# A second seven-product set in the first layer of a retention and feed-forward kernel on one Trainium2 core

## Chip, cores and metric

The kernel runs on one core of one Trainium2 chip. The metric is the device time of one execution in microseconds (us). Of the kernel before, ten executions are known.

## What is computed

A retention (linear attention with decay) over 8 batches, 8 heads, 576 positions and 64 dimensions gives a matrix of 4608 tokens by 512; a two-layer feed-forward net with a leaky ReLU of slope 0.01 follows.

```
scores = scale * q @ k.T            # per batch and head
ret    = (scores * Dmat) @ v        # Dmat = gamma_h ** (row - col), 0 above the diagonal
x      = ret, heads side by side    # (4608, 512)
h      = x @ w_in                   # (512, 2048)
g      = maximum(0.01 * h, h)
out    = g @ w_out                  # (2048, 512), float32
```

## The kernel before

**Tiling.** The 4608 tokens are 36 units of 128 tokens, or nine groups `g` of 512 tokens, four units each. The retention is done per unit `u` in two chunks of 64 positions: scores inside a chunk (masked), and a state matrix that is carried from chunk to chunk. There are nine chunks in a batch; chunk number 2u or 2u+1 modulo 9 says what `state` has to do: 0 is a copy, 8 is nothing, 3 and 7 take an addition and a scaling, the others one addition. In f16, TensorE does all the products.

**The order of the work is written by hand.** Every engine carries out its instructions in the order of the program's text; the code issues pieces of retention between pieces of the feed-forward net. `burst(u)` issues the scores of unit u and the outputs of unit u-1 on TensorE, then the evacuations: `masks` (VectorE, scores from PSUM times the mask, to f16), `state` (VectorE), `state_cast` (GpSimd), `own` (ScalarE) and `add` (VectorE), which give the columns `xT` of the net's input. `step(u)` is a burst, the loads of unit u+4 on SP's DMA queue, and `ahead(u+2)`: casts of k on ScalarE, of q and v on GpSimd, and the transposing DMA on SP. Once in a group `step` also has `sum_x`, four differences of `xT` on GpSimd.

**First layer.** A block `f` is 128 of the 2048 hidden columns for the group's 512 tokens: `h_block`, four matmuls of 512 columns into one PSUM buffer, then `leaky` on ScalarE. For the set of blocks 0, 1, 8 and 9 of groups 2 to 8, `h_seven` (from line 447) uses a Strassen-like scheme: a 2x2 split of the weights, of the contraction and of the tokens, with seven products of four 256-column matmuls in place of four blocks of four 512-column matmuls. It needs the sums of weights `w_sum` (made once by `sum_w_in` on VectorE), the sums of inputs from `sum_x`, and additions on VectorE (`plus`, line 468: `u2`, `v`, `h4`, `h5` and a second `h4`). Its first product `p1` is copied by ScalarE to `k1` (line 475), and then `p1` goes on accumulating in the same PSUM buffer. Four plain blocks, given in `fill`, lie between the products. I write p1b, p5b and p7b for the second product that goes into the buffer p1, p5 or p7.

**Second layer.** `seven` has the same scheme, each product 16 matmuls of 256 columns. Its sums of activations are made by `mix` on VectorE in 16 bits (line 554): four kinds, each for two halves `x` of the hidden columns; kinds 2 and 3 are written in place. Its p1 is copied to `k1` by ScalarE in `keep` (line 586), and `give` (line 600) adds and stores. The results of a product are written to SBUF tiles and go out by SP.

**Order in a group before the change:** `h_seven` with four plain blocks, a step, six plain blocks (with three mixes of half 0 after the third), a step, two plain blocks, three mixes of half 1, and then `seven`: p1, two mixes, a step, p1b, p6, p5, p7, a step, p5b, p7b. All products of both layers use one pool `acc` of four PSUM buffers, which are taken in turn; scores (`sc`) and outputs (`ot`) have a buffer each of their own. `m_pool` holds the copies and sums with one buffer for each name.

**Ahead of the groups**, units 0 to 7 are brought in with finer pieces: transposes of q and k on TensorE, which `turn` copies from PSUM by VectorE and `turn_act` by ScalarE (line 208). Group 0 is done without the scheme (`wide`), group 1 with the second layer's alone (`seven(1, ...)`).

Of the kernel before, what the change touches and what calls it, by code (L numbers as in the profile page):

```python
# [18 lines left out]
def kernel(  # L19
# [9 lines left out]
    nc = tc.nc  # L29
# [74 lines left out]
    w_in16 = const_pool.tile([P, NP, DFF], F16, name="w_in16")  # L104
    w_out16 = const_pool.tile([P, NF, DM], F16, name="w_out16")
    w_mix = const_pool.tile([P, 4, HF, HN], F16, name="w_mix")
    w_sum = const_pool.tile([P, 4, NP // 2, 2 * P], F16, name="w_sum")
    zst = const_pool.tile([P, NP, CH], F16, name="zst")
    idle = const_pool.tile([P, TOK], F16, name="idle")

    t32, qk16, v16, qkT, s16s, st16, sc_tiles, ot_tiles, xT = ({} for _ in range(9))
    last_load = {}
# [119 lines left out]
                        start=True, stop=True, skip_group_check=True,  # L232
                    )

    def masks(u):
        s16s[u] = b_pool.tile([P, 2, NP, CH], F16, name="s16")
        nc.vector.tensor_tensor(  # L237
            out=s16s[u],
            in0=sc_tiles[u][:, :, 0],
            in1=mask_sb.unsqueeze(1).unsqueeze(1).to_broadcast([P, 2, NP, CH]),  # L240
            op=MUL,
        )
# [145 lines left out]
    def g_tile(g):  # L388
        if g not in g_t:
            g_t[g] = g_pool.tile([P, NF, TOK], F16, name="gt")  # L390
        return g_t[g]

    def leaky(out, in_):
        nc.scalar.activation(out=out, in_=in_, func=mybir.ActivationFunctionType.Lrelu)  # L394

    def h_block(g, f):
        hps = acc_pool.tile([P, 1, TOK], FP, name="acc")
        h_mm(hps, 0, g, f, slice(0, TOK))
        leaky(g_tile(g)[:, f : f + 1, :], hps)
# [15 lines left out]

    def w_sub(i, j):
        return w_in16[:, 2 * j : 2 * j + 2, i * HF * P : i * HF * P + 2 * P]

    def x_sub(g, j, k):
        return xT[g][:, 2 * j : 2 * j + 2, k * HT : (k + 1) * HT]

    def sum_w_in(n):
        a, b, op = (
            (w_sub(1, 0), w_sub(1, 1), ADD),
            (w_sum[:, 0], w_sub(0, 0), SUB),
            (w_sub(0, 0), w_sub(1, 0), SUB),
            (w_sub(0, 1), w_sum[:, 1], SUB),
        )[n]  # L430
        nc.vector.tensor_tensor(out=w_sum[:, n], in0=a, in1=b, op=op)

    x_sums = {}

# [9 lines left out]
        ):  # L444
            nc.gpsimd.tensor_tensor(out=t[:, n], in0=a, in1=b, op=SUB)  # L445

    def h_seven(g, fill):

        r = {}
        t = x_sums[g]  # L450

        def product(name, lhs, rhs, fresh):
            if fresh:
                r[name] = acc_pool.tile([P, 2, HT], FP, name="acc")
            for n in range(2):
                for c in range(NP // 2):
                    nc.tensor.matmul(  # L457
                        out=r[name][:, n, :],
                        lhsT=lhs[:, c, n * P : (n + 1) * P],
                        rhs=rhs[:, c, :],  # L460
                        start=fresh and n == 0 and c == 0,
                        stop=c == NP // 2 - 1,
                        skip_group_check=True,
                    )

        def plus(name, a, b):
            r[name] = m_pool.tile([P, 2, HT], FP, name=name)
            nc.vector.tensor_tensor(out=r[name], in0=r[a], in1=r[b], op=ADD)  # L468

        def give(i, k, name):  # L470
            leaky(g_tile(g)[:, i * HF : i * HF + 2, k * HT : (k + 1) * HT], r[name])

        product("p1", w_sub(0, 0), x_sub(g, 0, 0), True)
        r["k1"] = m_pool.tile([P, 2, HT], FP, name="k1")
        nc.scalar.copy(out=r["k1"], in_=r["p1"])
        h_block(g, fill[0])
        product("p1", w_sub(0, 1), x_sub(g, 1, 0), False)
        give(0, 0, "p1")
        h_block(g, fill[1])
        product("p6", w_sum[:, 1], t[:, 1], True)  # L480
        plus("u2", "p6", "k1")
        product("p5", w_sum[:, 0], t[:, 0], True)
        plus("v", "p5", "u2")
        h_block(g, fill[2])
        product("p7", w_sum[:, 2], t[:, 2], True)
        plus("h4", "p7", "v")
        product("p5", w_sum[:, 3], x_sub(g, 1, 1), False)
        plus("h5", "p5", "u2")
        give(1, 1, "h4")
        h_block(g, fill[3])  # L490
        give(0, 1, "h5")
        product("p7", w_sub(1, 1), t[:, 3], False)
        plus("h4", "p7", "u2")
        give(1, 0, "h4")

# [28 lines left out]
    def w_part(a, b):  # L524
        return w_out16[:, a * HF : (a + 1) * HF, b * HN : (b + 1) * HN]
# [13 lines left out]
    def g_part(g, a, b):  # L539
        return g_t[g][:, b * HF : (b + 1) * HF, a * HT : (a + 1) * HT]  # L540
# [12 lines left out]
        )[n]  # L553
        nc.vector.tensor_tensor(out=z[:, fs], in0=a[:, fs], in1=b[:, fs], op=op)  # L554

    def seven(g, hooks, last=False):

        r = {}
        s = sums[g]

        def product(name, lhs, rhs, fresh):
            apart = last and name == "p7"
            if fresh:
                r[name] = [
                    acc_pool.tile([P, 1 if apart else 2, HN], FP, name="acc")
                    for _ in range(2 if apart else 1)
                ]
            order = (
                [(f, tb) for tb in range(2) for f in range(HF)]
                if last  # L570
                else [(f, tb) for f in range(HF) for tb in range(2)]
            )
            for n, (f, tb) in enumerate(order):
                nc.tensor.matmul(  # L574
                    out=r[name][tb][:, 0, :] if apart else r[name][0][:, tb, :],
                    lhsT=lhs[:, f, tb * P : (tb + 1) * P],
                    rhs=rhs[:, f, :],
                    start=fresh and (f == 0 if apart else n == 0),
                    stop=f == HF - 1,
                    skip_group_check=True,  # L580
                )

        def keep(name, of, plus=None):
            r[name] = m_pool.tile([P, 2, HN], FP, name=name)
            if plus is None:
                nc.scalar.copy(out=r[name], in_=r[of][0])  # L586
            else:
                nc.vector.tensor_tensor(out=r[name], in0=r[of][0], in1=r[plus], op=ADD)

        def give(a, b, of, plus=None):  # L590
# [21 lines left out]
            if r["n", a] == 2 and not (last and a == 1):  # L612
                store(g, a, r["o", a])

        plan = (
            ("p1", g_part(g, 0, 0), w_part(0, 0), True, lambda: keep("k1", "p1")),
            ("p1", g_part(g, 0, 1), w_part(1, 0), False, lambda: give(0, 0, "p1")),
            ("p6", s[:, 1], w_mix[:, 1], True, lambda: keep("u2", "p6", "k1")),
            ("p5", s[:, 0], w_mix[:, 0], True, lambda: keep("v", "p5", "u2")),
            ("p7", g_part(g, 1, 0), w_mix[:, 2], True, lambda: give(1, 1, "p7", "v")),  # L620
            ("p5", g_part(g, 0, 0), w_part(1, 1), False, lambda: give(0, 1, "p5", "u2")),
            ("p7", g_part(g, 1, 1), w_mix[:, 3], False, lambda: give(1, 0, "p7", "u2")),
        )
        if last:
            plan = (plan[0], plan[2], plan[1]) + plan[3:]
        for n, (name, lhs, rhs, fresh, then) in enumerate(plan):
            product(name, lhs, rhs, fresh)
            then()
            if n == 0:
                mix(g, 3, 0)  # L630
                mix(g, 3, 1)
            for f in hooks.get(n, ()):
                f()

# [126 lines left out]
    def burst(u, out=True):  # L763

        if u < NU:
            scores(u)
        if out:
            outputs(u - 1)
        if u < NU:
            masks(u)  # L770
            state(u, 0)
            state(u, 1)
            state_cast(u, pool_copy)
        if out:
            own(u - 1)
            add(u - 1)
# [62 lines left out]
    masks(6)  # L839
    cast_q(7, nc.vector)  # L840
    state(6, 1)
    cast_v(7, nc.vector)
    h_unit(5, 1)
    turn(7, 1)
    halves(1, (0, 4))
    outputs(6)
    own(6)
    turn(7, 0)
    add(6)
    state_cast(6, act_copy, (1,))  # L850
    halves(1, (0, 5))
# [27 lines left out]
    def early(u, n):  # L879
# [7 lines left out]
        3: lambda: mixes(1, 1),  # L887
        4: lambda: (burst(8, False), ahead(11), load(13)),
        7: lambda: mixes(1, 2),
        12: lambda: [sum_w_in(n) for n in range(4)],  # L890
        9: lambda: early(9, 12),
    }
    for n in range(16):
# [1 line left out]
        if n in at:  # L895
            at[n]()
    burst(10)
    seven(1, {0: [lambda: early(11, 13)], 4: [lambda: early(12, 14)]})

    rest = [f for i in range(2, HF) for f in (i, i + HF)]  # L900
    for g in range(2, NG):
        more = g < NG - 1
        h_seven(g, rest[:4])
        if more:
            step(4 * g + 5)
        for n, f in enumerate(rest[4:]):
            h_block(g, f)
            if n == 2:
                for m in range(3):
                    mix(g, m, 0)  # L910
            if more and n == 5:
                step(4 * g + 6)
        for m in range(3):
            mix(g, m, 1)
        seven(
            g,
            {0: [lambda: step(4 * g + 7)], 4: [lambda: step(4 * g + 8)]} if more else {},
            g == NG - 1,
        )


# [28 lines left out]
```

## Time and profile before

| what | value |
|---|---|
| median of 10 executions | 287.45 us |
| lowest, highest | 287.18, 290.26 us |
| profiled execution, its own time | 288.79 us |
| its span in the profile | 287.0 us |
| TensorE clock granted, mean | 0.994 of full speed |
| groups 2 to 7 in the profile | five of 28.80 to 28.86 us, the first (84.32 to 113.20) 28.88 |
| group 8 (from 257.34 us) | to the end, 29.7 us |

The profile is of one execution, the median of ten others. The rows in order of time give start, length, engine, line, operation, the tile written and the tiles read, shapes and how many instructions were merged into the row; in brackets stands the idle time of the engine ahead of it and what ended that. A matmul's length in the rows is longer than its spacing from the next, since matmuls are pipelined; spacing is taken from starts. PE is TensorE, DVE VectorE, ACT ScalarE, POOL GpSimd.

### The profile page before, as it was taken

To read this page: it belongs to the slowest core of one execution; us is meant where nothing else is said; L and a number is where in the kernel's file an instruction comes from. 1 tells how busy PE (TensorE), PEld (TensorE's weight loads), DVE (VectorE), ACT (ScalarE), POOL (GpSimd) and SP (SyncE) were. 2 spreads that over 40 slices of the span, in tenths; PEclk is the share of its full clock that TensorE was granted. 3 is DMA by queue.
4 is the path that set the end of the run, shared out by engine and by line. 5 is a ranking of instruction groups with operands and counts; after the bars stand their busy time and mean duration, and the time that the engine had idled before them with its cause. 6 is when DMAs were issued, how large, how long until landed. Compare 5 with 4: busy or idle time off the path is not lost.

```text
span 287.0 us, 9702 instructions
## 1 busy us (share of the span) xinstructions
PE 277.6 (97%) x4195; PEld 198.6 (69%) x4195; DVE 204.8 (71%) x336; ACT 145.0 (51%) x261; POOL 141.1 (49%) x152
## 2 busy tenths in 40 slices
PE   5989999999999999999999999999999999999994
PEld 1558888745886588658865886588648864886584
DVE  1785577958766896699668975997599659845352
ACT  3567776623327832783278326832683167316610
POOL 8979402483446536553656446545655564132000
PEclk9799999999999999999999999999999999999999
DMA  8999999699999997948894969478959351012004
GB/s 217 299 234 229 287 207 234 154 190 234 243 222 282 214 204 165 276 106 173 184 274 97 206 148 276 110 168 185 255 127 174 76 185 39 3 49 100 0 0 148
DMA packets 131739, 50.03 MB, mean 174 GB/s; under 512 B 121264, under 2 KB 126000, under 8 KB 131696
## 3 DMA queue, kind: packets, MB, share of 16 engines
q1 hardware_dynamic: 125392, 39.59, 60.5%
q0 software_dynamic: 6016, 9.70, 15.0%
q8 instruction: 33, 0.54, 0.8%
q10 hardware_dynamic: 288, 0.11, 0.1%
q14 instruction: 10, 0.08, 0.1%
HBM read 36.81 MB, written 9.44 MB: 161 GB/s over the span
## 4 chain that ended last, share of the span: by engine, by line
PE 91%; DVE 3%; ACT 2%; DMA 2%; issue 1%; SPq 0%; ACTq 0%; DVEq 0%
PE acc L380 35%; PE acc L574 34%; PE acc L457 8%; PE acc L510 5%; PE sc L219 2%; DMA t<-in_q_dram 2%; PE ot L295 1%; PE ot L306 1%; PE sc L228 1%; PE acc L640 1%; PE acc L201 1%; ACT k L586 1%; ACT qkT L208 1%; PE acc L328 1%; DVE qk L176 0%
## 5 line engine op out<-in xcount | busy, mean ns | idle before, releaser
L380 PE MATMUL acc<-xT,w_in 128*128 128x512 f16 (+2 forms) x656 | 110.5, 317 | 0.4 <-ACT xT L348 0.3
L394 ACT ACTIVATE gt<-acc 128x512 f16<-128x512 f32 x123 | 71.4, 597 | 28.3 <-PE acc L380 27.8
L380 PEld LDWEIGHTS <-w_in 128*128 128x128 f16 x656 | 57.2, 98 | 34.0 <-issue 0.4
L574 PEld LDWEIGHTS <-gt 128*128 128x128 f16 x640 | 61.7, 98 | 9.5
L277 POOL CAST st<-s 128x512 f16<-128x512 f32 x21 | 12.8, 610 | 68.7 <-DVE s L261 40.5
L574 PE MATMUL acc<-w_out,gt 128*128 128x256 f16 x384 | 45.9, 273 | 0.4
L176 POOL TENSOR_TENSOR qk<-t,cs 128x512 f16<-128x512 f32 x28 | 32.5, 1162 | 20.2 <-DMA t<-in_q_dram 19.5
L362 ACT COPY own<-ot 128x512 f32<-128x512 f32 x33 | 19.2, 581 | 42.6 <-PE ot L306 36.5
L180 POOL TENSOR_TENSOR v<-t,cs 128x512 f16<-128x512 f32 x28 | 34.8, 1242 | 0.0
L574 PE MATMUL acc<-w_mix,gt 128*128 128x256 f16 x256 | 30.6, 273 | 0.0
L574 PE MATMUL acc<-w_mix,mix 128*128 128x256 f16 x256 | 29.6, 273 | 0.0
L574 PEld LDWEIGHTS <-mix 128*128 128x128 f16 x256 | 24.9, 98 | 3.2 <-DVE mix L554 0.2
L237 DVE TENSOR_TENSOR s<-sc,cs 128x512 f16<-128x512 f32 x34 | 23.2, 682 | 5.0 <-PE sc L228 5.0
L367 DVE TENSOR_TENSOR xT<-ot,own 128x512 f16<-128x512 f32 x33 | 22.6, 683 | 5.1 <-ACT own L362 5.1
L173 ACT CAST qk<-t 128x512 f16<-128x512 f32 x36 | 22.3, 620 | 4.6 <-DMA t<-in_k_dram 4.6
L554 DVE TENSOR_TENSOR mix<-gt 128x1024 f16<-128x1024 f16 x16 | 14.4, 904 | 7.8 <-ACT gt L394 7.8
L554 DVE TENSOR_TENSOR mix<-mix,gt 128x1024 f16<-128x1024 f16 x16 | 18.9, 1188 | 0.5
L445 POOL TENSOR_TENSOR x_sum<-xT 128x512 f16<-128x512 f16 x14 | 16.1, 1153 | 5.6 <-DVE xT L367 5.6
L261 DVE TENSOR_TENSOR s<-sc,s 128x256 f32<-128x256 f32 x37 | 15.5, 419 | 2.8 <-PE sc L228 2.2
L468 DVE TENSOR_TENSOR u<-acc,k 128x512 f32<-128x512 f32 x7 | 4.8, 691 | 17.1 <-PE acc L457 17.1
L600 DVE TENSOR_TENSOR osb<-acc,u 128x512 f32<-128x512 f32 (+1 forms) x17 | 11.2, 656 | 7.9 <-PE acc L574 7.9
L445 POOL TENSOR_TENSOR x_sum<-xT,x_sum 128x512 f16<-128x512 f16 x14 | 16.2, 1154 | 0.5
(74 smaller groups left out, 351.8 us busy)
## 6 DMA issues: line engine op xcount, KB each, us to landing
out_dram<-osb SPq DMA_DIRECT2D x17, 512.0 KB, 3.7
t<-in_k_dram SPq DMA_DIRECT2D x27, 256.0 KB, 4.0
t<-in_q_dram SPq DMA_DIRECT2D x26, 256.0 KB, 4.2
t<-in_v_dram SPq DMA_DIRECT2D x25, 256.0 KB, 4.5
w_in<-in_moe_w_in_dram POOLq DMA_DIRECT2D x8, 256.0 KB, 6.0
w_out<-in_moe_w_out_dram POOLq DMA_DIRECT2D x4, 512.0 KB, 10.1
t<-in_v_dram POOLq DMA_DIRECT2D x7, 256.0 KB, 5.7
t<-in_q_dram POOLq DMA_DIRECT2D x6, 256.0 KB, 5.6
```

Source lines behind the costliest of these rows:

```text
L173: nc.scalar.copy(out=qk16[u][:, 1], in_=t32[u, 1])
L176: eng.tensor_tensor(out=qk16[u][:, 0], in0=t32[u, 0], in1=decay(u, 0), op=MUL)
L180: eng.tensor_tensor(out=v16[u], in0=t32[u, 2], in1=decay(u, 1), op=MUL)
L237: nc.vector.tensor_tensor(out=s16s[u], in0=sc_tiles[u][:, :, 0], in1=mask_sb.unsqueeze(1).unsqueeze(1).to_broadcast([P, 2, NP, CH]), op=MUL,)
L362: nc.scalar.copy(out=owns[u], in_=ot_tiles[u][:, :, 0:NP].rearrange("q j c t -> q c j t"))
L367: nc.vector.tensor_tensor(out=x_of(u).rearrange("q (c g) t -> q c g t", g=2), in0=ot_tiles[u][:, :, NP : 2 * NP].rearrange("q g (c j) t -> ...
L380: nc.tensor.matmul(out=hps[:, n, :], lhsT=w_in16[:, c, f * P : (f + 1) * P], rhs=xT[g][:, c, ts], start=(c == 0), stop=(c == NP - 1),)
L394: nc.scalar.activation(out=out, in_=in_, func=mybir.ActivationFunctionType.Lrelu)
L445: nc.gpsimd.tensor_tensor(out=t[:, n], in0=a, in1=b, op=SUB)
L457: nc.tensor.matmul(out=r[name][:, n, :], lhsT=lhs[:, c, n * P : (n + 1) * P], rhs=rhs[:, c, :], start=fresh and n == 0 and c == 0, stop=c ...
L554: nc.vector.tensor_tensor(out=z[:, fs], in0=a[:, fs], in1=b[:, fs], op=op)
L574: nc.tensor.matmul(out=r[name][tb][:, 0, :] if apart else r[name][0][:, tb, :], lhsT=lhs[:, f, tb * P : (tb + 1) * P], rhs=rhs[:, f, :], s ...
```

## The change

Three edits.

1. `seven` is split into `first` (p1 and its copy to `k1`) and `others`. `first` is issued ahead of the last product of the set before it, so that block 15 and a step lie between p1 and p1b.
2. For unit 7, the copy of q's transposes moves from VectorE to ScalarE, and `cast_v(7)` moves behind the copy of k's.
3. Blocks 4, 5, 12 and 13 of groups 2 to 8 become a second `h_seven`, so that two sets and eight plain blocks make the sixteen (before, one set and twelve plain blocks). `w_sum` has a second half, whose four sums VectorE makes inside `seven(1)`. The steps 4g+5 and 4g+6 move into the middle of the two sets (`middle`, between `v` and the third fill). From unit 13 on, `masks` is done by a ScalarE copy to f16 and a GpSimd product with an f16 mask, which a VectorE copy makes once. For the last group `seven` had p1, p6, p1b; now it has p1, p1b, p6, as the other groups.

```
-    def masks(u):
+    def masks(u, aside=False):
         s16s[u] = b_pool.tile([P, 2, NP, CH], F16, name="s16")
+        if aside:
+            nc.scalar.copy(out=s16s[u], in_=sc_tiles[u][:, :, 0])
+            nc.gpsimd.tensor_tensor(
+                out=s16s[u],
+                in0=s16s[u],
+                in1=mask16.unsqueeze(1).unsqueeze(1).to_broadcast([P, 2, NP, CH]),
+                op=MUL,
+            )
+            return
...
-    def h_seven(g, fill):
+    def h_seven(g, f, fill, middle=None):
...
-        product("p1", w_sub(0, 0), x_sub(g, 0, 0), True)
+        product("p1", w_sub(f, 0, 0), x_sub(g, 0, 0), True)
         r["k1"] = m_pool.tile([P, 2, HT], FP, name="k1")
         nc.scalar.copy(out=r["k1"], in_=r["p1"])
-        h_block(g, fill[0])
-        product("p1", w_sub(0, 1), x_sub(g, 1, 0), False)
+        fill[0]()
+        product("p1", w_sub(f, 0, 1), x_sub(g, 1, 0), False)
         give(0, 0, "p1")
-        h_block(g, fill[1])
-        product("p6", w_sum[:, 1], t[:, 1], True)
+        fill[1]()
+        product("p6", w[:, 1], t[:, 1], True)
         plus("u2", "p6", "k1")
-        product("p5", w_sum[:, 0], t[:, 0], True)
+        product("p5", w[:, 0], t[:, 0], True)
         plus("v", "p5", "u2")
-        h_block(g, fill[2])
-        product("p7", w_sum[:, 2], t[:, 2], True)
+        if middle is not None:
+            middle()
+        fill[2]()
+        product("p7", w[:, 2], t[:, 2], True)
         plus("h4", "p7", "v")
-        product("p5", w_sum[:, 3], x_sub(g, 1, 1), False)
+        product("p5", w[:, 3], x_sub(g, 1, 1), False)
         plus("h5", "p5", "u2")
         give(1, 1, "h4")
-        h_block(g, fill[3])
+        fill[3]()
         give(0, 1, "h5")
-        product("p7", w_sub(1, 1), t[:, 3], False)
+        product("p7", w_sub(f, 1, 1), t[:, 3], False)
         plus("h4", "p7", "u2")
         give(1, 0, "h4")
...
+        def first():
+            product("p1", g_part(g, 0, 0), w_part(0, 0), True)
+            keep("k1", "p1")
+
+        def others(hooks):
+            mix(g, 3, 0)
+            mix(g, 3, 1)
+            for f in hooks.get(0, ()):
                 f()
...
         if u < NU:
-            masks(u)
+            masks(u, u > 12)
...
-    cast_v(7, nc.vector)
     h_unit(5, 1)
     turn(7, 1)
+    cast_v(7, nc.vector)
     halves(1, (0, 4))
     outputs(6)
     own(6)
-    turn(7, 0)
+    turn_act(7, 0)
     add(6)
...
+    others(
+        {
+            0: [lambda: early(11, 13)],
+            2: [lambda: sum_w_in(4, 0), lambda: sum_w_in(4, 1)],
+            3: [lambda: sum_w_in(4, 2), lambda: sum_w_in(4, 3)],
+            4: [lambda: early(12, 14)],
+        }
+    )
...
+        h_seven(g, 0, [block(2), block(10), block(3), block(11)], at_step(5))
+        mix(g, 0, 0)
+        mix(g, 1, 0)
+        h_seven(g, 4, [block(6), block(7), block(14), first], at_step(6))
+        mix(g, 2, 0)
+        h_block(g, 15)
+        for n in range(3):
+            mix(g, n, 1)
+        others({0: [at_step(7)], 4: [at_step(8)]} if more else {})
```

## Prediction

> **What bounds the kernel now.** I read the page's busy shares first, then the busy time per stretch for one steady group of 512 tokens, then the order of time of each engine inside it. In the steady part TensorE has no room left; the page's first part, and one group's stretch (length, then busy time and count of TensorE, its weight loads, VectorE (DVE), ScalarE (ACT) and GpSimd (POOL)):
>
> ```profile
> PE 277.6 (97%) x4195; PEld 198.6 (69%) x4195; DVE 204.8 (71%) x336; ACT 145.0 (51%) x261; POOL 141.1 (49%) x152
> ```
> ```profile
> 113.20:142.04 28.84, 28.84 (x446) 20.55 (x444) 22.74 (x35) 15.08 (x27) 15.61 (x17) 1.00 0.80 186
> ```
>
> A group takes 28.84 us with TensorE busy throughout and VectorE for 22.74. Next, in order of time, TensorE's rows (start, length), then VectorE's, then ScalarE's, from the end of the seven-product set to the second layer:
>
> ```profile
> 117.55 0.60 PE L457 MATMUL acc<-x_sum,w_sum 128*128 128x256 f16 x4
> 118.04 0.60 PE L457 MATMUL acc<-xT,w_sum 128*128 128x256 f16 x4
> 118.48 1.03 PE L380 MATMUL acc<-xT,w_in 128*128 128x512 f16 x4
> 119.34 0.60 PE L457 MATMUL acc<-x_sum,w_in 128*128 128x256 f16 x4
> 119.87 0.32 PE L219 MATMUL sc<-qkT 64*64 64x64 f16 x16
> ...
> 120.52 5.36 PE L380 MATMUL acc<-xT,w_in 128*128 128x512 f16 x24
> 125.80 0.32 PE L219 MATMUL sc<-qkT 64*64 64x64 f16 x16
> ...
> 130.82 1.91 PE L574 MATMUL acc<-w_out,gt 128*128 128x256 f16 x16
> ```
> ```profile
> 117.30 0.69 DVE L468 TENSOR_TENSOR v<-acc,u 128x512 f32<-128x512 f32 x1
> 118.19 0.69 DVE L468 TENSOR_TENSOR h<-acc,v 128x512 f32<-128x512 f32 x1 [0.19 <-PE acc L457]
> 118.79 0.68 DVE L468 TENSOR_TENSOR h<-acc,u 128x512 f32<-128x512 f32 x1
> 120.05 0.69 DVE L468 TENSOR_TENSOR h<-acc,u 128x512 f32<-128x512 f32 x1 [0.57 <-PE acc L457]
> ...
> 130.12 1.42 DVE L554 TENSOR_TENSOR mix<-mix,gt 128x1024 f16<-128x1024 f16 x1
> 131.46 0.68 DVE L554 TENSOR_TENSOR gt<-gt 128x1024 f16<-128x1024 f16 x1
> ```
> ```profile
> 118.91 0.63 ACT L394 ACTIVATE gt<-h 128x512 f16<-128x512 f32 x1 [0.56 <-DVE h L468]
> 119.54 0.60 ACT L394 ACTIVATE gt<-acc 128x512 f16<-128x512 f32 x1
> 120.04 1.37 ACT L394 ACTIVATE gt<-h 128x512 f16<-128x512 f32 x2
> 121.31 0.57 ACT L362 COPY own<-ot 128x512 f32<-128x512 f32 x1
> ...
> 130.18 0.59 ACT L586 COPY k<-acc 128x512 f32<-128x512 f32 x1 [1.21 <-PE acc L574]
> ```
>
> See three things. 24 matmuls of 512 columns take 5.28 us (120.52 to 125.80): 0.88 a block of four. The first-layer set's last product (p7b, 119.34) is followed on other engines by a tail: sum 120.05 to 120.74, its leaky copy until 121.41. Today an attention burst and blocks in other buffers follow, so nobody waits for that tail. And the second layer's p1b starts at 130.82, only when the copy k of p1 ends (130.77), though the attention burst ahead of it began at 130.02 and takes 0.64 (119.87 to 120.52): 0.16 us lost per group.
>
> **What the Trainium skill says.** "TensorE: Matmul & The Clock Gate", Back-to-back issue gap: a warm matmul costs columns/2.4 ns plus a fixed 2.5 ns, so 28 short ones save a little less than their columns against 16 long ones. The trace agrees: 220 ns (5.28/24) and 109 ns (32 matmuls in 3.50 us, 132.56 to 136.06). "Perfetto Trace Analysis", Per-engine timelines: ScalarE and VectorE are strict FIFOs. The trace agrees: their rows stand in program order, and the leaky copy at 119.54 goes ahead of one whose sum was ready earlier. "SBUF — State Buffer", Who interferes with whom: VectorE with two SBUF inputs blocks against GpSimd (POOL) reads. The trace agrees: mix sums take 0.69 us in the last group with POOL idle, 1.42 at 130.12 beside a POOL cast.
>
> **The change part by part.**
> *Second set by seven, products.* The set takes 113.20 to 119.80 with four blocks in it: 6.60 - 4 x 0.87 = 3.11 us for seven products, against 4 x 0.88 = 3.52. Gain 0.41 x 7 groups = 2.9 us, all on TensorE.
> *First second-layer product moved up.* Block 15 and the burst now lie between p1 and p1b, over 1.5 us against 0.84 of latency and copy. Gain 0.16 x 6 groups = 1.0 (the last group has no burst). It also removes 1.75 us of cover between block 15 and the mixes, below.
> *Unit 7.* In the chain at 42.24 to 45.18 us, VectorE has two transposes' copies and cast_v ahead of add(6). One copy (0.33 us start to start) goes to ScalarE, which after own(6) (43.08) can do it by 44.2, when scores(7) comes up. h_unit(6) starts 0.3 earlier. Gain 0.3; TensorE has no gap after it that would eat it until 58.8.
> *The wait that the second set adds.* Its p1 is copied to k1 by ScalarE, and p1b accumulates into the same PSUM buffer, so p1b waits for the copy. In the first set ScalarE is idle then. In the second, k1 stands in ScalarE's queue behind the first set's tail. From p7b's start: the last sum starts at +0.71 (120.05), ends +1.40, its leaky copy lets the next instruction in at +1.97 (121.31), k1 lasts 0.59 to +2.56, and 0.05 later (as at 130.77 to 130.82) p1b may start: +2.61. TensorE gets there after p7b 0.46, p1 0.43 and block 6 0.88: +1.77. Stall 0.84 x 7 groups = **5.9 us**. Queued behind are only blocks in other buffers; the whole TensorE queue waits.
> *Burst 4g+5 inside the first set.* VectorE now has state operations and add between v and h4. From the group's start: v at 4.10, state at 4.70; two state operations put add at 5.49, h4 at 6.09 to 6.78, h5 to 7.38. TensorE reaches p7b at 6.85 (just free) and the second set's p1, which takes p5's buffer (four buffers in turn), at 7.31: about 0.1 us of wait, counted with what the queue passes on. The chunks 2u, 2u+1 modulo 9 give the operations: one for u=13, two for 17, 25, 29, three for 21 and 33 (a scaled chunk costs one more, 0.45). Three operations: h4 ends at 7.23, p7b waits 0.42, p1 0.14 more: 0.55. Sum 3 x 0.1 + 2 x 0.55 = 1.4 us. The second set's burst is covered by p1 of the second layer, 1.75 us.
> *Masks aside.* VectorE loses 4 x 0.68 and gains 5 x 0.69 a group: +0.7 on 22.74. ScalarE gains 4 copies of 0.58, POOL four products. No row shows such a product; the nearest are the f16 difference (1.15) and the casts (1.04 to 1.49). I take 1.15: POOL goes to about 20 of 29 us. The masked scores are needed a burst later, 5.6 us or more: hidden. On ScalarE the copy waits for the scores; behind it stand own, cast_k and block 3's leaky copy, whose buffer is needed only four allocations on: 0. On SP the transpose of unit u+2 waits for POOL's cast, now 1.15 later; loads and stores queue behind it, and it has two bursts' time: 0. On POOL the products stand ahead of sum_x, whose second piece today ends at 144.17, 0.49 before its use at 144.66; but states come 0.6 earlier without masks on VectorE, so I take 0, at worst 0.4 a group.
> *Mixes between the sets.* Two mixes run on VectorE from 8.5 to at most 11.5 from the group's start (1.56 and 1.42 when blocked); the second set's first sum, u2, wants VectorE at 11.5, after the k1 wait: 0, at worst 0.3.
> *Mixes without p1's cover.* Block 15's leaky copy waits for the second set's tail and starts 1.97 after p7b, ends 2.57; mixes at 2.61 and, 0.74 later, 3.35. POOL then starts its mask product, so the second mix takes 1.42: until 4.77. Second-layer p6 needs it at its fifth weight: 0.46 + 0.88 + 0.71 + 1.75 + 0.88 = 4.68. Wait 0.1. Behind it: v needs three more mixes (1.8), states, add, u; it ends at 9.4 (9.8 with three operations), p5b needs it at 9.7. Together 1.0 us in six groups; zero if POOL is quiet, 4.8 (0.8 a group) if the first mix is blocked too.
> *Last group.* No burst: p1b needs block 15's half at 0.46 + 0.88 + 0.77 = 2.1, has it at 2.6: 0.5, against 0.13 today at p6 (1.88 instead of 1.75 us). Loss 0.4.
> *Four more weight sums and the mask's copy*, on VectorE at 76 to 80 us in gaps of about 1 us: 0.1, at worst 0.3. The loads that steps issue on SP move up with them by up to 3 us; no TensorE wait on a load shows after 45 us: 0.
>
> Sum: gains 2.9 + 1.0 + 0.3 = 4.2; losses 5.9 + 1.4 + 1.0 + 0.4 + 0.1 = 8.8. Net **+4.6 us**. The profiled execution took 288.79 (span 287.0): 293.4 expected; the median shown is 1.34 below it, so **292.0**.
>
> **Rivals.** *Faster: the k1 wait doesn't bind.* If the tail took under 1.77 us instead of 2.61, or the copy found its way ahead of it, only 4.2 - 0.9 of small waits is left: 284.1. For it: VectorE gets lighter masks; against: every link of the tail is a row, and ScalarE is in order. *About the same: only the tail counts.* Without the burst's and the mixes' waits, and with a tail 0.3 us shorter, losses are 3.8 + 0.5: 287.5. *Much slower: VectorE becomes the bound.* It is busy 23.5 of some 29 us in order; the mixes blocked by POOL in each group and sum_x late by 0.3 add 4.8 - 1.0 + 1.8: 297.6. For it: 1.42 against 0.69 us for a mix; against: POOL has a gap where the first mix falls.
>
> **How the numbers follow.** Slower as reckoned 0.58, by its own bounds 289.3 (no burst or mix waits, 8.8 - 2.4) to 294.5; much slower 0.17; the same 0.12; faster 0.13. A measurement of this kernel tells about 0.5% from no change (286.0 to 288.9). The range leaves out the faster case and the top of the slowest: 287.0 to 296.5. Faster 0.13, same 0.12, slower 0.75.
>
> **What would show it.** Right: the second set's second product starts about 0.8 us late, at the end of a ScalarE copy at L475's successor, seven times, as the largest TensorE wait; the sets' products total 0.4 us less per group than four blocks; the 0.16 before second-layer p1b is gone. Wrong: second-set p1b starts straight after block 6, or TensorE's largest idle time stands before p6 or p5b of the second layer (then VectorE), or before the x_sum products (then POOL).

## The result and the profile after

| | before | after |
|---|---|---|
| median of executions | 287.29 us (31) | 295.03 us (9) |
| lowest, highest | 286.75, 290.26 us | 294.05, 295.86 us |
| profiled execution, its own time | 288.79 us | 294.05 us |
| its span | 287.0 us | 291.9 us |
| group 2 starts | 84.32 us | 82.33 us |
| from there to the end of the span | 202.7 us | 209.6 us |

The ratio is 1.0252, with an interval of 1.0229 to 1.0274: slower by 7.7 us. The profiled execution of before began its groups late (84.32; in nearly all profiles of this study 82.3 to 83.7): from 5 to 10 us its TensorE clock was granted at 0.75 and from 10 to 15 at 0.91, where after's profile has 1.00 in both. And after's profile is the shortest of its nine. So I compare the part that the change rebuilds, from group 2's start to the end: **+6.9 us** (209.6 - 202.7).

Counted from one start of a group's first product to the next, groups 2 to 7 take 28.88, 28.84, 28.92, 28.93, 28.87 and 28.58 us in before (mean 28.84), and 29.33, 29.65, 30.58, 29.88, 29.76 and 29.73 in after. (The table of before gives five of them as 28.80 to 28.86; its boundaries are up to 0.26 us off these starts.)

First the engines' shares, then one group of after (columns as in the same views of before):

```profile
PE 276.1 (95%) x4279; PEld 204.8 (70%) x4279; DVE 211.9 (73%) x352; ACT 158.4 (54%) x292; POOL 161.0 (55%) x175
```
```profile
111.67:141.31 29.64, 28.83 (x459) 21.54 (x457) 22.14 (x36) 17.26 (x32) 19.43 (x21) 1.00 0.80 178
```

TensorE is busy 28.83 of 29.64 us here, where before it had no gap at all. The gap stands in one place. TensorE's order of time at the second set, and then at the second layer:

```profile
118.63 0.61 PE L470 MATMUL acc<-x_sum,w_in 128*128 128x256 f16 x4
119.08 0.60 PE L470 MATMUL acc<-xT,w_in 128*128 128x256 f16 x4
119.52 1.03 PE L390 MATMUL acc<-xT,w_in 128*128 128x512 f16 x4
121.29 0.60 PE L470 MATMUL acc<-xT,w_in 128*128 128x256 f16 x4 [0.75 <-ACT k L488]
...
129.84 1.92 PE L588 MATMUL acc<-w_out,gt 128*128 128x256 f16 x16
131.59 3.89 PE L588 MATMUL acc<-w_mix,mix 128*128 128x256 f16 x32
135.32 1.91 PE L588 MATMUL acc<-w_mix,gt 128*128 128x256 f16 x16
```

The rows are the first set's p7b, the second set's p1, block 6, and p1b. Block 6 is handed over by 119.52 + 0.87 = 120.39; p1b starts at 121.29, 0.90 later. (A row's own length overlaps the next by some 0.16 us, so the bracket shows 0.75; I take spacings.) Below them are the second layer's p1b (no bracket: the 0.16 us of before is gone), then p6 and p5 in one row, then p7. From p6's start to p7's is 3.73 us where before it was 3.50. ScalarE in the same stretch:

```profile
119.15 0.58 ACT L404 ACTIVATE gt<-acc 128x512 f16<-128x512 f32 x1
119.62 1.14 ACT L404 ACTIVATE gt<-h 128x512 f16<-128x512 f32 x2
120.66 0.58 ACT L488 COPY k<-acc 128x512 f32<-128x512 f32 x1
```

The copy `k1` begins at 120.66 although its data left TensorE at about 119.7. Ahead of it in the queue is the leaky copy of the first set's last sum. That copy ends at 121.24, and p1b starts 0.05 later. In the table of TensorE's waits (total, times, longest) the first of these two is now the largest; before had no entry for a first-layer product:

```profile
PE acc L470 <- ACT k L488: 5.1, 7, 0.7
PE acc L470 <- DVE h L481: 1.6, 3, 1.0
```

The second entry is p7b's wait for the sum `h4` inside the first set. Its longest case, group 4, all engines in one order of time:

```profile
146.63 1.16 POOL L240 TENSOR_TENSOR s<-s,idle 128x512 f16<-128x512 f16 x1
...
146.99 1.08 DVE L275 TENSOR_TENSOR s<-stmp,cs 128x256 f32<-128x256 f32 x1
147.99 0.68 DVE L377 TENSOR_TENSOR xT<-ot,own 128x512 f16<-128x512 f32 x1
...
148.59 0.67 DVE L481 TENSOR_TENSOR h<-acc,v 128x512 f32<-128x512 f32 x1
...
149.32 0.28 PE L470 MATMUL acc<-x_sum,w_in 128*128 128x256 f16 x1 [1.02 <-DVE h L481]
```

VectorE's scaling of a state (L275) takes 0.42 us when alone. Here it runs beside GpSimd's new mask product and takes 1.08. That pushes `add` and `h4` back, and p7b with them. It depends on which of the two starts first. In group 7 VectorE has the same three state operations in another order, and the scaling starts 0.03 us ahead of the product. It keeps its length, the product takes 1.42 us instead of 1.16, and p7b waits 0.59 us where in group 4 it waits 1.17:

```profile
236.82 0.42 DVE L275 TENSOR_TENSOR s<-stmp,cs 128x256 f32<-128x256 f32 x1
236.85 1.42 POOL L240 TENSOR_TENSOR s<-s,idle 128x512 f16<-128x512 f16 x1
```

Where the product is first, as at 146.99 and at four more scalings (169.45, 185.84, 199.73, 215.98), the scaling ends 0.28 or 0.29 us after the product does, whatever its length comes to (0.57 to 1.08 us).

### The profile page after: what moved, and what is told of

Same layout as the page of the kernel before. It is cut to its first block, busy times and chain, and to the rows that moved or that the text cites. A ratio compares the mean times of both kernels' runs of the same rounds, so it can differ in the third digit from the quotient of the medians.

```text
span 291.9 us, 9901 instructions
## 1 busy us (share of the span) xinstructions
PE 276.1 (95%) x4279; PEld 204.8 (70%) x4279; DVE 211.9 (73%) x352; ACT 158.4 (54%) x292; POOL 161.0 (55%) x175
## 4 chain that ended last, share of the span: by engine, by line
PE 66%; DVE 15%; ACT 7%; POOL 4%; DMA 4%; issue 2%; DVEq 0%; ACTq 0%; POOLq 0%
PE acc L588 24%; PE acc L390 19%; PE acc L470 12%; ACT gt L404 6%; PE acc L525 5%; DVE mix L569 5%; POOL t L134 3%; DVE h L481 3%; PE sc L220 2%; DMA w_in<-in_moe_w_in_dram 2%; DMA qkT<-qk 2%; DVE xT L377 1%; DVE s L271 1%; DVE s L275 1%; ACT k L488 1%
## 5 line engine op out<-in xcount | busy, mean ns | idle before, releaser
L390 PE MATMUL acc<-xT,w_in 128*128 128x512 f16 (+2 forms) x544 | 88.7, 304 | 0.6 <-DMA w_in<-in_moe_w_in_dram 0.3
L404 ACT ACTIVATE gt<-acc 128x512 f16<-128x512 f32 x102 | 60.0, 597 | 18.0 <-PE acc L390 16.5
L390 PEld LDWEIGHTS <-w_in 128*128 128x128 f16 x544 | 46.2, 98 | 17.7 <-issue 0.7
L240 POOL TENSOR_TENSOR s<-s,idle 128x512 f16<-128x512 f16 x23 | 27.3, 1186 | 42.0 <-ACT s L239 42.0
L239 ACT CAST s<-sc 128x512 f16<-128x512 f32 x23 | 13.4, 584 | 35.9 <-PE sc L229 35.9
L404 ACT ACTIVATE gt<-h 128x512 f16<-128x512 f32 x42 | 25.9, 628 | 12.5 <-DVE h L481 11.8
L481 DVE TENSOR_TENSOR u<-acc,k 128x512 f32<-128x512 f32 x14 | 9.7, 692 | 26.6 <-PE acc L470 26.6
L470 PEld LDWEIGHTS <-w_sum 128*128 128x128 f16 x224 | 21.9, 98 | 9.1 <-issue 0.5
L470 PEld LDWEIGHTS <-w_in 128*128 128x128 f16 x168 | 15.9, 97 | 15.6 <-issue 7.1
L481 DVE TENSOR_TENSOR h<-acc,u 128x512 f32<-128x512 f32 x28 | 19.2, 685 | 8.4 <-PE acc L470 8.4
L470 PE MATMUL acc<-x_sum,w_sum 128*128 128x256 f16 x168 | 22.9, 272 | 0.3 <-POOL x_sum L457 0.3
```

The source lines that it names most:

```text
L240: nc.gpsimd.tensor_tensor(out=s16s[u], in0=s16s[u], in1=mask16.unsqueeze(1).unsqueeze(1).to_broadcast([P, 2, NP, CH]), op=MUL,)
L390: nc.tensor.matmul(out=hps[:, n, :], lhsT=w_in16[:, c, f * P : (f + 1) * P], rhs=xT[g][:, c, ts], start=(c == 0), stop=(c == NP - 1),)
L470: nc.tensor.matmul(out=r[name][:, n, :], lhsT=lhs[:, c, n * P : (n + 1) * P], rhs=rhs[:, c, :], start=fresh and n == 0 and c == 0, stop=c ...
```

## The experiments

**Theory A** is the prediction's: `k1` stands in ScalarE's queue behind the first set's tail, and TensorE waits for it seven times; the smaller waits are the rest. **Rival B**: VectorE sets the time, through the burst inside the first set, the masks' way round and the mixes.

**e1: `k1` first.** The leaky copy of the first set's last sum, and the two mixes, are issued behind the second set's `k1`: `h_seven` calls `between` right after that copy. VectorE keeps its order, as it has nothing between the mixes and u2; ScalarE's changes.

```
-        give(1, 0, "h4")
+        if f:
+            give(1, 0, "h4")
+        return lambda: give(1, 0, "h4")
...
-        h_seven(g, 0, [block(2), block(10), block(3), block(11)], at_step(5))
-        mix(g, 0, 0)
-        mix(g, 1, 0)
-        h_seven(g, 4, [block(6), block(7), block(14), first], at_step(6))
+        tail = h_seven(g, 0, [block(2), block(10), block(3), block(11)], at_step(5))
+        def between():
+            tail()
+            mix(g, 0, 0)
+            mix(g, 1, 0)
+        h_seven(g, 4, [block(6), block(7), block(14), first], at_step(6), between)
```

> The changed kernel with one order altered: the first set's last leaky copy, give(1, 0), is issued behind the second set's copy k1 (and the two mixes between the sets behind it), so that ScalarE does k1 first. Each engine has the same instructions. Theory A (k1 waits in ScalarE's queue): the wait before the second set's p1b, 0.84 to 0.91 us in each of seven groups in the changed kernel, sum 6.2, falls to about 0.15; about 5.2 us less, 289.8. Theory B (VectorE is the bound, the k1 wait only stands where the time would be lost anyway): VectorE's work is unaltered, so the time comes back as a wait before p6, p5b or p7b and the median stays within 1 us of 295.

Measured: 290.37 us, ratio to before 1.0078 (1.005 to 1.0106), 5.0 us less than after (1.0252 - 1.0078, of 287.3). TensorE's order of time, block 6 and p1b:

```profile
120.03 1.03 PE L390 MATMUL acc<-xT,w_in 128*128 128x512 f16 x4
121.28 0.60 PE L470 MATMUL acc<-xT,w_in 128*128 128x256 f16 x4 [0.23 <-ACT k L488]
```

The wait falls from 0.90 to 0.38 (120.03 + 0.87 = 120.90, to 121.28) in this group; all together its rows fall from 5.1 to 1.1 us, by spacings from 6.2 to 2.1. From group 2 to the end the trace is 4.0 us shorter than after's (205.6 against 209.6). A holds. Its size is 4 us in the trace and 5.0 by the ratios, whose intervals leave about 1 us either way (beside e1 to e4 before's own median was 287.96; in plain medians e1 is 4.7 below after). The wait was to fall to about 0.15 in every group; it does in the first and the last (0.10) and stays at 0.38 in five.

**e2: the step between the sets.** Step 4g+5 leaves the first set and stands between the two. If B is right and the burst inside the set costs most, this is faster.

```
-        h_seven(g, 0, [block(2), block(10), block(3), block(11)], at_step(5))
+        h_seven(g, 0, [block(2), block(10), block(3), block(11)])
+        if more:
+            step(4 * g + 5)
```

> The changed kernel with step 4g+5 between the two sets instead of in the middle of the first. It gives TensorE 0.65 us more to do between p7b and the second set's p1b, and ScalarE three more copies ahead of k1. Theory A: k1 now starts about 1.5 us later and p1b waits about 1.6 us a group instead of 0.9 in six groups, +4.2; the waits before p7b in the first set (2.3 us) go; 297. Theory B (what matters is VectorE's load in the first set, and cover on TensorE): 2.3 us from p7b and up to 0.65 a group from p1b come off, 289 to 293.

Measured: 297.69 us, ratio 1.035 (1.029 to 1.0409). The same two rows:

```profile
124.21 1.03 PE L390 MATMUL acc<-xT,w_in 128*128 128x512 f16 x4
126.67 0.60 PE L470 MATMUL acc<-xT,w_in 128*128 128x256 f16 x4 [1.44 <-ACT k L488]
```

The wait grows to 1.59 us (124.21 + 0.87 = 125.08): the step's ScalarE copies now stand ahead of `k1` too. The p7b waits it removes (2.3 us in the sum) don't pay for that. B fails as the main cause.

**e3: no second set.** Edits 1 and 2 alone: block order as a plain loop, masks on VectorE, no second half of `w_sum`.

```
-        h_seven(g, 4, [block(6), block(7), block(14), first], at_step(6))
-        mix(g, 2, 0)
-        h_block(g, 15)
+        for n, f in enumerate((4, 12, 5, 13, 6, 14, 7, 15)):
+            if f == 15:
+                first()
+            h_block(g, f)
+            if n == 2:
+                for m in range(3):
+                    mix(g, m, 0)
+            if more and n == 5:
+                step(4 * g + 6)
```

> Only the first two edits: first product of the second layer ahead of block 15, and unit 7's q transposes by ScalarE; one set of seven, the masks on VectorE, steps where they were. Expected from the prediction's terms: 0.16 x 6 = 1.0 and 0.3 us gained, about 0.4 lost in the last group (p1b ahead of p6) and 0.1 a group at p6, whose mix loses 1.75 us of cover: 286.8, between 286.0 and 287.6. If the cover of p1 was what hid the mixes, 1 us a group is lost: 293.

Measured: 286.37 us, ratio 0.9936 (0.991 to 0.9961). TensorE's order of time at the second layer's p1b:

```profile
128.37 0.32 PE L220 MATMUL sc<-qkT 64*64 64x64 f16 x16
...
129.01 1.92 PE L588 MATMUL acc<-w_out,gt 128*128 128x256 f16 x16
```

p1b follows 0.64 us after the burst's start, the burst's own length, with no bracket. Groups 3 to 6 take 28.70 to 28.80 us, against 28.84 to 28.93. The two small edits gain about what they were reckoned at (286.8 was expected); all of the loss is edit 3's. This is the one version in the study whose interval lies wholly under 1.

**e4: one more copy.** The tail's last leaky copy and its instruction are issued twice in the first set: one ScalarE instruction more ahead of `k1`, on the same data.

```
         give(1, 0, "h4")
+        if f == 0:
+            give(1, 0, "h4")
```

> The changed kernel with the last leaky copy of the first set, give(1, 0), done twice: one more ScalarE instruction ahead of k1, seven in all, the same values. Theory A: each adds the spacing of such copies, 0.53 us, to the wait of p1b: 7 x 0.53 = 3.7, 298.7. Theory B or any other in which ScalarE's queue has slack at this place: no more than 0.5, 295.0 to 295.5.

Measured: 298.91 us, ratio 1.0374 (1.0345 to 1.0403). The bracket at p1b is 1.35 to 1.41 in place of 0.69 to 0.75: 0.66, about one leaky copy, is added each time, 4.6 us in seven. The trace from group 2 to the end is longer by as much (214.1 against 209.6); by the ratios it is 3.5 us (1.0374 - 1.0252, of 287.3), by plain medians 3.9. What stands ahead of `k1` on ScalarE costs its full length on TensorE.

**e5: masks on VectorE.** `masks(u, u > 12)` becomes `masks(u)`; everything else as after.

> The changed kernel with the masks by VectorE again, as before, and nothing else altered. Theory A with VectorE's queue as a second limit: in the first set the mask adds 0.6 us ahead of h4, so p7b waits 0.6 more in six groups (3.6 us, passed on to k1's wait, which starts from p7b), against about 2.4 that come back because no mask product of GpSimd blocks VectorE (0.2 a group at p6, 0.6 at p7b of group 4, 0.4 at x_sum of group 5): 296, between 294.5 and 298. If the masks' way round is what costs (theory C: GpSimd's products block VectorE more than they relieve it): 292.

Measured: 295.67 us, ratio 1.0284 (1.0266 to 1.0301). Without GpSimd's products no scaling is blocked (the longest L275 is 0.43 us, against up to 1.08 beside these products in after), and p6 no longer waits (3.49 us to p7). In exchange VectorE does four masks more per group, and p7b waits 0.44 to 0.97 us in five groups, 3.3 us by its rows against 1.6. So the masks' way round is worth next to nothing in the changed kernel (1.0284 against 1.0252, with intervals that overlap): what it spares at p7b it costs at the scaling and at p6. `sum_x` is late by 0.42 us in one group either way, in group 6 here and in group 5 of after.

**e6: both orders.** e1, and step 4g+5 behind `k1` and the tail, so that neither a burst inside the set nor a copy ahead of `k1` is left.

```
-        tail = h_seven(g, 0, [block(2), block(10), block(3), block(11)], at_step(5))
+        tail = h_seven(g, 0, [block(2), block(10), block(3), block(11)])
         def between():
             tail()
+            if more:
+                step(4 * g + 5)
             mix(g, 0, 0)
```

> Two orders altered at once: k1 of the second set ahead of the first set's last leaky copy, as in the run that had that alone, and step 4g+5 behind k1 and that copy, ahead of block 6, out of the first set. In the run with the step between the sets it made k1 later; here it stands behind k1 in ScalarE's queue and ahead of p1b on TensorE. Theory A: neither p7b nor p1b waits; from the run with k1 first, 2.3 us of p7b and 7 x 0.35 of p1b come off, 4.7: ratio to the kernel before 0.992, 285.5. Theory B: the step's state operations and add, now ahead of the two mixes and u2, make p6's sum late: p5b or the burst waits instead and no more than 1.5 us comes off: 289.

Measured: 295.31 us, ratio 1.0294 (1.0272 to 1.0316). Both theories missed. The waits at p1b and p7b are gone, and a new one, together as long, stands at the second set's p5b, for `v`. TensorE, then VectorE in group 3:

```profile
124.88 0.60 PE L470 MATMUL acc<-x_sum,w_sum 128*128 128x256 f16 x4
127.71 0.49 PE L470 MATMUL acc<-xT,w_sum 128*128 128x256 f16 x3 [2.23 <-DVE v L481]
```
```profile
121.31 0.42 DVE L274 TENSOR_TENSOR stmp<-sc,s 128x256 f32<-128x256 f32 x1 [1.43 <-ACT s L239]
121.84 0.95 DVE L275 TENSOR_TENSOR s<-stmp,cs 128x256 f32<-128x256 f32 x1
...
123.32 1.49 DVE L573 TENSOR_TENSOR mix<-gt 128x1024 f16<-128x1024 f16 x1
124.84 1.42 DVE L573 TENSOR_TENSOR mix<-mix,gt 128x1024 f16<-128x1024 f16 x1
...
126.96 0.69 DVE L481 TENSOR_TENSOR v<-acc,u 128x512 f32<-128x512 f32 x1
```

Three things stand in a row on VectorE ahead of `v`. The first state operation waits 1.43 us for ScalarE's mask copy. Scaling takes 0.95 and the mixes 1.49 and 1.42 us, all beside GpSimd. Then come u2 and `v`. Rival B, refuted as the cause of after's loss, is the next limit once A's is lifted.

**e7: block 15 early.** e6, with block 15 as the second set's fourth fill and the second layer's p1 and two mixes ahead of p7b (six groups).

> As the run with both orders, and in six groups block 15 as the fourth fill, then the first second-layer product with mixes of kind 2 (half 0) and kind 0 (half 1) issued ahead of p7b, so that the mix that p6 waits for starts earlier. Theory: the wait of about 0.2 a group at p6 goes, 1.3 in all, and p1b may wait up to 0.2 a group for blocks 12 and 13, which have lost block 15's cover: 0.5 to 1.3 less than with both orders alone, ratio 0.988. If the mixes blocked by GpSimd push h4 and its leaky copy back: the same as both orders alone or up to 1 us more.

Measured: 299.01 us, ratio 1.0404 (1.0384 to 1.0425): a miss. The waits for `v` are the same (7.4 us by rows, longest 2.2), and the second layer's p1 now waits halfway for leaky copies (3.0 us by rows, up to 1.18): it stands closer behind the blocks and halves that it reads. Part of the profile's length is clock: in group 3, behind the longest wait for `v` (2.23 us), TensorE was granted 0.50 of full speed from 130 to 132 us, and the second layer's p1 took 3.41 us (128.93 to 132.34) instead of 1.75. In e6 a wait of the same length left the clock at 1.00.

**e8: e7 with masks on VectorE.** `masks(u)` in e7.

> As the run with block 15 early, with the masks by VectorE. Where no wait stands on VectorE's chain any more, 2.7 us more a group on it (about 25.5 of 28.4 busy) should cost little if its idle time can be used, and much if the order leaves none: theory A says the masks' way round is not what makes the gain, within 1.5 us of the run with block 15 early; theory B says 4 us or more.

Measured: 297.13 us, ratio 1.0339 (1.0323 to 1.0355), 1.9 us less than e7. `v` is waited for 4.1 instead of 7.4 us, while waits for leaky copies and for the second layer's `k1` grow (4.2 and 2.7 us). With this order the masks' way round costs time. The run doesn't tell ScalarE's copy from GpSimd's product.

**e9: step at the first set's start.** e1, with step 4g+5 behind the first set's own `k1`, where ScalarE and VectorE have room.

```
-        tail = h_seven(g, 0, [block(2), block(10), block(3), block(11)], at_step(5))
+        tail = h_seven(g, 0, [block(2), block(10), block(3), block(11)], None, at_step(5))
```

> As the run with k1 first, and step 4g+5 moved from the middle of the first set to the first set's start, behind its own k1: VectorE is idle there for 2.4 us ahead of u2, and ScalarE for 2.7 us ahead of k1. Theory A with VectorE's queue as second limit: the waits before p7b (2.3 us in all) go and those of the second set's p1b fall from 0.38 to about 0.1 (7 x 0.28 = 2.0), 0.1 a group may come at the first set's p5, whose buffer is freed behind the step's copies; from 1.0078 to 0.995, 285.8. If the step's work only moves the wait, as in the run with both orders, where v came late by 1.0 to 2.2 us: 289 or more.

Measured: 288.88 us, ratio 1.004 (1.0022 to 1.0057). The waits at p7b and for `k1` are gone and that for `v` is 0.4 us by rows, but scores now wait for the transposing DMA, 2.1 us at 85.10 and 0.4 at 144.33: the burst has moved ahead of the transfer it needs. The first of these waits costs more than its length. Behind it TensorE was granted 0.54, 0.50 and 0.50 of full speed in the three microseconds from 85 to 88, four matmuls of 512 columns took 1.68 us (86.10 to 87.78) instead of 0.87, and the group takes 32.28 us where the next takes 28.65.

**e10: second tail behind block 15.** In e9, six groups issue the second set's tail after block 15, so that its leaky copy goes ahead of the tail's.

```
-        tail2()
+        if not more:
+            tail2()
         mix(g, 2, 0)
         h_block(g, 15)
+        if more:
+            tail2()
```

> As the run with the step at the start, and in six groups the second set's last leaky copy issued behind block 15's, so that ScalarE does block 15 first and the mix that p6 waits for starts 0.4 us earlier, ahead of GpSimd's next mask product. Theory: the 0.22 a group before p6 goes, 1.3 us in all, and p1b still has blocks 12 and 13 in time: 284.5, ratio 0.990. If p6's wait comes from the mix's length beside GpSimd and not from its start: no difference from the run with the step at the start.

Measured: 287.19 us, ratio 0.9994 (0.9975 to 1.0013). p6 no longer waits, and the waits for the transposing DMA are down to 1.3 us. TensorE at p6 and p7, and in another group at scores:

```profile
101.17 3.66 PE L590 MATMUL acc<-w_mix,mix 128*128 128x256 f16 x32
104.66 1.91 PE L590 MATMUL acc<-w_mix,gt 128*128 128x256 f16 x16
...
140.76 0.32 PE L220 MATMUL sc<-qkT 64*64 64x64 f16 x16 [1.12 <-DMA qkT<-qk]
```

From 101.17 to 104.66 are 3.49 us again. The first group takes 28.34 us (82.31 to 110.65): half a microsecond below before's. The transfer behind the wait at 140.76 had been issued at 135.05, 5.7 us earlier; such transposes took 2.7 to 5.7 us to land in this trace, 3.7 at the median. Group 4 (139.04) still takes 29.54 us; 1.28 of that is this wait.

**e11: burst after block 2.** e10 with the burst and its loads one block later and the casts in the middle of the set.

> As the run with the second tail behind block 15, but burst 4g+5 and its loads stand behind block 2 instead of ahead of it, and the casts and transpose of unit 4g+7 in the middle of the first set. The last run's groups took 28.34 us where no transposed q and k was awaited, yet its median stood 1.8 us above its lowest time, and its profile has 1.1 us before the scores of burst 4g+5, whose transpose is issued 5.7 us ahead of them. If that transpose is what is left, 0.88 us more ahead of it takes about half of it: 286.3, ratio 0.996. If not: 287.2 as before.

Measured: 287.34 us, ratio 0.9994 (0.9976 to 1.0013). Nothing is gained. One transpose is still waited for (1.27 us at 85.09), and `v` in group 4 (0.95).

**e12: loads later.** e11, with the loads of step 4g+8 behind the second layer's p5b, so that they don't lie ahead of the transposes.

> As the run with the burst behind block 2, and the loads that step 4g+8 issues on SP stand behind p5b, so that they do not follow the transpose of unit 4g+9 at once. If those loads are what makes that transpose land in 5.7 us instead of the median 3.7, the wait before the scores goes and the spread of the times with it: 285.6, ratio 0.993. If the transpose is late because it is issued late: no difference from the run with the burst behind block 2.

Measured: 287.08 us, ratio 0.9988 (0.9973 to 1.0003). In the trace no matmul waits for a transpose any more, and the longest takes 5.4 us to land (6.2 in e11). `v` in group 4 is waited for as in e11; the scaling ahead of it started behind a difference of `sum_x` on GpSimd, and took 1.12 us:

```profile
143.31 1.16 POOL L457 TENSOR_TENSOR x_sum<-xT,x_sum 128x512 f16<-128x512 f16 x1
143.64 1.12 DVE L275 TENSOR_TENSOR s<-stmp,cs 128x256 f32<-128x256 f32 x1
...
146.80 0.60 PE L470 MATMUL acc<-xT,w_sum 128*128 128x256 f16 x4 [0.99 <-DVE v L481]
```

In that trace TensorE's scores follow one another, burst 4g+5 to the next group's, after 28.33, 28.45, 29.48 and 28.45 us: but for group 4, half a microsecond less than before's 28.84, which is what the products and the early p1 save (0.41 + 0.16). From group 2's start to the end it takes 201.5 us, 1.1 less than before. The median moves by 0.2, which is within its interval. In this trace some of the gain is lost ahead of the groups: group 2 starts at 83.36, in e10's at 82.31, and the clock was granted at 0.75 from 10 to 15 us and at 0.90 from 15 to 20, in e10's at 1.00. **Open:** where the executions at the median lose the rest. It is not the clock alone, as those of e12 from 287.19 to 287.73 had 1.00. Those of e10 go from 285.37 to 289.61 us, its profile (285.75) being one of the shortest; a longer landing of the transposes in the others would fit, but no trace of such an execution is here.

## Why the prediction was right, and where its sizes were off

The direction and the mechanism hold: 292.0 us was forecast, within 287.0 to 296.5, and 295.03 came. By its waits the likeliest case ("slower as reckoned") is the one that happened; by its size it is not, as its own upper bound, 294.5, was passed by 0.5. (Its lower bound, 289.3, is 289.6 by its own sum, 292.0 - 2.4; nothing rests on it.) The median lies about midway between 292.0 and the rival in which VectorE becomes the bound (297.6), but the waits tell the two apart: `k1` makes up 6.2 of 10.7 us of losses, and the waits that come through VectorE 4.0, where that rival had them at 8. Term by term, from group 2 to the end:

| step of the prediction | forecast, us | measured, us |
|---|---|---|
| products of the second set | -2.9 | -2.9 |
| 0.16 ahead of second-layer p1b | -1.0 | -1.0 |
| wait for `k1`, seven times | +5.9 | +6.2 |
| burst inside the first set, at p7b | +1.4 | +2.3 |
| mixes without p1's cover, at p6 | +1.0 | +1.3 |
| `sum_x` late | 0 | +0.4 |
| last group | +0.4 | +0.45 |
| sum | +4.8 | +6.75 (spans: +6.9) |

A wait is measured here as the spacing of two starts less the time of the matmuls between them.

- **Products.** In the last group, which has no burst, the first set takes 6.58 us with four blocks of 0.87 in it, so 3.1 us for seven products as forecast; the second set gives the same with three blocks, its wait and a second-layer p1 in it. The spacing formula that the prediction takes from "TensorE: Matmul & The Clock Gate", Back-to-back issue gap, is given there for an isolated matmul; for a stream the page has about 131 ns at 512 columns. In this kernel the measured 220 and 109 ns decide for the formula.
- **The `k1` wait.** The forecast came link by link: sum, leaky copy, copy, 2.61 us from p7b against TensorE's 1.77. Measured are 0.84 in group 2 and 0.85 in the last, 0.90 or 0.91 in the others. e1, e2 and e4 show the cause: order changed, wait falls; a copy added, it rises by about that copy. The rival "the `k1` wait doesn't bind" is out.
- **The burst in the first set is the term that failed**, by 0.9 us. The step said that two or three state operations and `add` decide when `h4` comes, each by its length alone. Group 7, where the scaling started ahead of GpSimd's product, bears that out: p7b waited 0.59 us where 0.55 was forecast. Group 4 shows otherwise: the scaling took 1.08 instead of 0.42 behind the mask product, and p7b waited 1.17 us. That is 0.6 of the 0.9; most of the rest is group 6 (0.36 against 0.1), where `v` began 0.46 us late for a reason that no run shows. "SBUF — State Buffer", Who interferes with whom, says that a VectorE instruction with two SBUF inputs contends with a GpSimd instruction that reads SBUF; I used that for the mixes and not for the scaling, which reads `stmp` and a factor, both in SBUF. The trace agrees (1.08 against 0.42 us), and e5, without the products, has no L275 above 0.43 us.
- **Masks aside at nothing** was wrong for the same reason: I asked whether GpSimd and ScalarE had time, not what they hold up on VectorE. "PSUM — Partial Sum Buffer", PSUM bank collisions raise a hardware error, asks for semaphores between engines by bank and quadrant of PSUM, not by address. The state operations read another part of the tile that ScalarE's mask copy reads, and they start 0.03 us after the end of that copy: for 0.34 us VectorE waited for it at 168.92 in after, for 1.43 in e6, where the copy stood behind `k1` and the tail in ScalarE's queue. Before, both were VectorE's and nobody waited. By e5, though, the masks on VectorE would have cost as much in this order.
- **`sum_x` at nothing** failed for want of room. The 0.49 us that the prediction read ahead of its second piece's use is group 4's. In groups 5 and 6 of before that piece ends at 173.61 and 202.49, and the product that reads it starts at 173.66 and 202.53. In group 5 of after the wait of 0.34 us and a scaling of 0.95 put `add`, and with it `sum_x`, 0.4 us later against the group's start; e5 has the same delay in group 6 without either.
- **The mixes** came out at 0.22 us in six groups, not 0.1 plus what is queued behind (the second mix took 1.52 us, not 1.42); e5 and e10 each remove it, by taking GpSimd's product or the tail out of the way.
- **Unit 7.** From the first block behind unit 6's scores to the first that reads unit 6's columns: 4.80 us before (40.38 to 45.18), 4.46 after. The 0.34 us (forecast 0.3) is there, and is given back before group 2: from the later of these rows to group 2's start, 39.14 us before and 39.46 after.
- **The profiled execution, in part by luck.** The working ended at 293.4 us for it, and 294.05 came. But from group 2 on the terms were 2.1 us short (4.8 against the spans' 6.9), and what made up for it is that before's profile began its groups 2.0 us later than after's (84.32 against 82.33), which the prediction did not reckon with. Between the medians the difference is 7.74 us, 0.8 more than from group 2 on; why after's other executions are longer than its profiled one (294.05 against a median of 295.03) no trace shows.

## What to carry to other kernels

Before an accumulation is continued in a PSUM buffer that another engine copies first, write down what stands ahead of that copy in its engine's queue, and add the whole chain that feeds it: here the order of one copy and one leaky copy was worth 4 to 5 us of 295 (e1). Work handed from VectorE to GpSimd and ScalarE is to be priced at VectorE too: in these traces its scaling, which reads two operands from SBUF, stretched from 0.42 to as much as 1.08 us behind a GpSimd product, and its operations on the same PSUM tile waited for ScalarE's read. When one queue's wait is lifted, look for the next before building on the gain: after `k1` came `v`, and after `v` the transposing DMA.

## What was not expected of the hardware

- VectorE's scaling of 128x256 float32 took 0.42 us alone, and in after 0.57 to 1.08 where a GpSimd mask product had started first (1.22 behind a cast at 58.23). The wait is inside the instruction's own row, not ahead of it, so a table of waits doesn't show it. Where the scaling started first, by 0.03 or 0.05 us, the product's row grew instead, from 1.16 to 1.42 and 1.40 us.
- The transposing DMA's landing time varies by a factor of two: it took 2.7 to 5.7 us from issue to landing in one trace (e10), and the two that TensorE waited for there took 5.7 and 5.2.
- A wait of 2.1 us on TensorE was in e9 followed by over three microseconds at about half the clock, which cost some 1.5 us more; one of 2.2 us was so in e7 and not in e6. What decides it stays open.
